# A fused attention and gated-MLP kernel: strided tile statistics, bias rows on another queue, operand sums in other places

## The chip, the cores and the metric

The kernel runs on one core of a Trainium2 chip. Its time is the device time of one launch in microseconds (us), taken as the median of several runs. A core has TensorE (PE, matrix products; PEld are its weight loads), VectorE (DVE), ScalarE (ACT), GpSimd (POOL) and SyncE (SP). Each has its own queue of instructions and takes them in order. ScalarE and SyncE also issue transfers (DMAs) from their queues: a transfer that must wait holds up whatever stands behind it on that engine. Engines wait for each other through semaphores.

## The reference

Two blocks with residuals, on x of 2048 tokens by 1024:

```python
h  = x + A(layernorm(x))          # 32 heads, 4 segments of 512 tokens, causal softmax in a segment,
                                  # plus a memory of the earlier segments, mixed by sigmoid(beta); then wo
h2 = h + B(layernorm(h))

def B(x):                         # F = 3584, Fh = 1792
    z  = gelu(x @ w_in)           # 2048 x 3584
    z1 = z[..., :Fh]
    z2 = layernorm(z[..., Fh:])   # over the 1792 features of a token
    g  = einsum('ts,sf->tf', w_sp, z2) + b_sp[:, None]     # w_sp is 2048 x 2048
    return (z1 * g) @ w_out       # 1792 x 1024
```

All inputs and the output are bf16. The change touches block B and nothing of A.

## The kernel before

**How it is built.** All operations go through a recorder (class _Recorder). It keeps the program's order on each engine and finds the waits itself: for each operand it looks up the cells of memory that it covers, 32 bytes of a partition each in SBUF (GRAN = 32), a whole bank of 2 KB in PSUM, and lets an instruction wait for the last writer or the readers of each cell. So two small tensors in one cell wait for each other though they share no byte, and a bank of PSUM is given back only when its reader has ended. There is no scheduler: the order of the Python calls is the order on each engine.

**Memory.** One arena holds everything at hand-chosen offsets. The first bytes hold constants of the attention (an identity at 0, an index table at 256, beta and gates from 768), dead after it; from there on small tensors of block B are laid out one after another (b3): ZST, ZMV, ZRS (statistics of z2, one entry for each tile of 128 tokens), SQ, SQZ, SQY (maxima or sums of squares for the f16 scales), TOT and TOP (scratch of a scale), SC and INV (a scale and its inverse), BSQ (squares of the bias rows).

**Stages of block B**, with their place in the profiled execution:

1. z2 (about 320 to 405 us). z2_group computes 128 tokens by 448 features of z; z2_gelu (ScalarE) writes it, z2_stats (VectorE) takes its statistics, and after the fourth part of a tile bn_aggr writes ZMV and GpSimd makes the inverse deviation ZRS by a power. The list todo gives the order of the groups; at(q, ...) hangs other work on the q-th group: sums of squares of w_sp (sp_norm), maxima of the weights of z1 (wz_norm), a scale (scale_of(1)), f16 copies of these weights (wz_half), and operand sums (hn_sum, sz_sum).
2. z1 (405 to 492 us). The product is done by Strassen's scheme in Winograd's form with two halves in each direction, 7 products for 8. Its operands are f16 and some are sums of blocks: hn_sum (VectorE, tensors HT, in the profile ht or z1x) of the activations, sz_sum (GpSimd, sz) of the weights. z1_step(g, k) is one product, g from 0 to 13 and k from 1 to 7; a list sorted by offs runs them in the order k = 6, 5, 1 of the next g, 7, 2, 3 of the last g, 4. on(g, k, ...) hangs other work on a step: z2_apply (normalises a tile of z2), scale_of(0) (the scale of w_sp), loads of w_sp (sp_load), f16 copies (sp_part), operand sums t1, t2, t3 (sp_sum).
3. First gating stage, gate(0), 492 to 577 us: the product of the first 1024 rows of w_sp with z2 by the same scheme, for g from 0 to 6 two columns of 128 features. p1 and p2 are the two products of one block of the result, the others accumulate in the banks bb and bc; stt (VectorE) reads a bank, scales, adds the bias, out multiplies by z1. s_sum makes operand sums of z2, copy1 (ScalarE) and two sums on GpSimd make the parts that several blocks share.
4. Output of the first 1024 tokens (577 to 633 us): 16 units of 128 tokens by 512 columns, 14 matmuls each. fin_load brings the residual into one of four buffers FIN; out_unit adds the product (fin on VectorE) and stores it. Both transfers are on ScalarE's queue, and the load for unit n + 2 waits for the store of unit n - 2 from the same buffer. Beside the units VectorE prepares w_sp for the second stage (sp_half, sp_sum), ScalarE squares w_out (wo_norm, in the profile t4h) and the bias rows (brow_sq, t4h too), and from the sums of squares come two scales: scale_y (YS, INVY) and scale_w (SCW, INVO). Each is a matmul of SQB with ones (total), a reduction on VectorE, a power on GpSimd and some operations of one column.
5. Second gating stage, gate(1), 633 to 719 us, as the first, for the other 1024 rows; each1(g, k) hangs the operands of the last stage on it: ScalarE's scaled copies of w_out (ob_scale) and VectorE's sums of them (ob_sum t1, t2, t3).
6. Output of the second 1024 tokens (719 to 767 us), again by the scheme: o_prod are the products, y_sum the operand sums sy of the gated values, o_adds GpSimd's sums of residual and shared part (ot), o_stt VectorE's reads of the banks. For g = 0 most of y_sum is done at the end of gate(1) for six of seven features; the last feature (lo = 6) follows when the last block is there.

**Lines that the steps touch:**

```python
        q.dma_start(FIN[k][:, 0:w], out2d[tc * 128:(tc + 1) * 128, lo:lo + w])     # fin_load
        if n == 9:
            brow_sq()
            scale_y()
            pool.tensor_copy(SQB[:, 0:8], SQY[:, 0:8])
        if n == 11:
            scale_w()
```

In this loop unit n's load, products, add and store are issued first, then wo_norm(n - 1) for n from 1 to 8, then the work of that n. In gate, each block g issues: products t2 and t1, stt of t2's bank, s_sum 4, 1 and 2, p1, each(g, 0), product t3, p2, each(g, 1), two stt, out, s_sum 3, stt and out of the next block's p1 and p2, product t4, each(g, 2), stt, out, product b22, stt, out, each(g, 3).

## Time and profile before

| | before |
|---|---|
| median of 13 runs | 768.63 us (761.83 to 770.74) |
| profiled execution: whole time | 768.99 us |
| profiled execution: span from first to last instruction | 767.3 us |
| mean granted TensorE clock | 0.996 |
| VectorE busy, 570 to 586 / 640 to 680 / 700 to 720 us | 9.01 of 16 / 36.46 of 40 / 18.86 of 20 |
| GpSimd busy, 390 to 420 us | 26.88 of 30 |

A time here is where something lies in the span. In rows of the timeline the number in brackets is the idle time of the engine just before the instruction, and behind the arrow what ended it. An instruction's duration as shown for TensorE includes about 0.16 us in which the next one already runs: products of 8 matmuls start every 1.73 us and are shown with 1.89. All operations bear the line of the recorder's helper (L210), so groups are told apart by tile names: zt are the sums of z1, tmp_u and tmp_s1b those of the gating stages, ss, sy, t1h to t4h, ht and sz operand sums, fin the output units.

### The profile page before, as it was taken

How to read it: one execution, taken by the hardware profiler on the slowest of the kernel's cores; microseconds unless marked ns; L12 is line 12 of the kernel's file. 1: busy time of each engine (PE TensorE's matmuls, PEld its weight loads, DVE VectorE, ACT ScalarE, POOL GpSimd, SP SyncE). 2: the span in 40 equal slices, each digit the busy share in tenths (PEclk: the TensorE clock that was granted, in tenths of full speed). 3: DMA queues.
4: the chain of work that ended last, by engine and by line, in shares of the span. 5: the costliest groups of instructions: out<-in, count | busy, mean ns of one | idle time of the engine just before them, and what ended most of it. 6: DMA issues, size and time to landing. Idle time of an engine off the chain costs nothing.

```text
span 767.3 us, 13442 instructions
## 1 busy us (share of the span) xinstructions
PE 748.0 (97%) x5401; PEld 358.2 (47%) x5470; DVE 576.5 (75%) x1016; ACT 422.9 (55%) x519; POOL 294.7 (38%) x447
## 2 busy tenths in 40 slices
PE   8999999999999999999999999999999979999898
PEld 4445555555454455455554444444444434444344
DVE  5586589768974675759866986998882755999986
ACT  6777877787777778146975789532230615300000
POOL 2574556555653333100079987412120001212242
PEclk9999999999999999999999999999999989999999
DMA  9654556353425231887620054500039830001111
GB/s 303 171 154 90 97 77 132 83 98 85 97 57 132 77 74 42 222 215 229 194 83 1 0 102 84 143 1 1 1 74 210 245 109 8 0 1 56 62 49 56
DMA packets 136784, 75.09 MB, mean 98 GB/s; under 512 B 98065, under 2 KB 126481, under 8 KB 136721
## 3 DMA queue, kind: packets, MB, share of 16 engines
q1 hardware_dynamic: 129472, 67.40, 36.2%
q10 hardware_dynamic: 7248, 6.82, 3.3%
q8 instruction: 43, 0.70, 0.4%
q14 instruction: 21, 0.16, 0.1%
HBM read 42.74 MB, written 8.39 MB: 67 GB/s over the span
## 4 chain that ended last, share of the span: by engine, by line
PE 75%; DVE 15%; issue 4%; POOL 3%; DMA 2%; ACT 1%; ACTq 0%; DVEq 0%; POOLq 0%
PE ps L210 75%; DVE tmp_u L210 2%; DVE z1x L210 2%; DVE ss L210 2%; DVE stats L210 1%; DVE zt L210 1%; POOL sz L210 1%; POOL zrs L210 1%; DMA out_dram<-fin 1%; DMA wv<-in_A_wv_dram 1%; DVE hch L210 1%; DVE sy L210 1%; DVE otok L210 0%; DVE fin L210 0%; DVE pqk L210 0%
## 5 line engine op out<-in xcount | busy, mean ns | idle before, releaser
L210 ACT ACTIVATE e<-ps 128x2048 bf16<-128x2048 f32 (+1 forms) x96 | 152.7, 1590 | 41.7 <-PE ps L210 41.5
L210 POOL TENSOR_SCALAR_AFFINE_SELECT e<-e 128x512 bf16<-128x512 bf16 x128 | 90.6, 720 | 131.9 <-ACT e L210 131.9
L210 PE MATMUL ps<-win,hnT 128*128 128x448 bf16 x512 | 98.4, 352 | 0.0
L210 POOL TENSOR_TENSOR tmp_s1b<-tmp_s,brow 128x512 f32<-128x512 f32 x28 | 33.9, 1212 | 133.8 <-DVE tmp_u L210 55.4
L210 PEld LDWEIGHTS ps<-win,hnT 128*128 128x128 bf16 x512 | 49.6, 98 | 46.3 <-issue 0.2
L210 PE MATMUL ps<-xnT,wk 128*128 128x512 bf16 x233 | 59.6, 380 | 1.2
L210 PE MATMUL ps<-wv,xnT 128*128 128x512 bf16 x255 | 59.4, 380 | 0.7 <-DMA wv<-in_A_wv_dram 0.4
L210 DVE TENSOR_TENSOR zt<-ps,zt 128x512 f32<-128x512 f32 x70 | 47.5, 687 | 15.3 <-PE ps L210 12.7
L210 PE MATMUL ps<-wo,oT 128*128 128x512 bf16 x254 | 57.7, 380 | 0.1
L210 PE MATMUL ps<-xnT,wq 128*128 128x512 bf16 x226 | 54.0, 379 | 1.6
L210 PE MATMUL ps<-w_out,z1T 128*128 128x512 bf16 x219 | 50.2, 390 | 0.3
L210 ACT ACTIVATE z<-ps 128x448 bf16<-128x448 f32 x60 | 30.8, 544 | 35.2 <-PE ps L210 35.2
L210 PEld LDWEIGHTS ps<-v,e 128*128 128x128 bf16 x1280 | 38.8, 96 | 14.0 <-issue 6.5
L210 DVE BATCH_NORM_STATS2 zst<-z 128x6 f32<-128x448 bf16 x64 | 37.8, 608 | 8.9 <-ACT z L210 8.8
L210 DVE RECIPROCAL rd<-ps 128x16 f32<-128x16 f32 x32 | 8.0, 250 | 47.1 <-PE ps L210 46.9
L210 PE MATMUL ps<-v,e 128*128 128x33 bf16 x1280 | 42.2, 178 | 0.0
L210 ACT ACTIVATE tmp_s<-ps,invy 128x512 f32<-128x512 f32 x7 | 4.8, 687 | 67.3 <-POOL tmp_s1b L210 36.9
L210 ACT ACTIVATE z1T<-zt,inv 128x512 bf16<-128x512 f32 x42 | 29.7, 719 | 16.2 <-DVE zt L210 16.1
L210 PEld LDWEIGHTS ps<-wo,oT 128*128 128x128 bf16 x256 | 24.1, 98 | 27.5
L210 PEld LDWEIGHTS ps<-xnT,wk 128*128 128x128 bf16 x256 | 22.6, 98 | 29.9 <-issue 5.0
L210 POOL TENSOR_TENSOR sz<-wzh 128x512 f16<-128x512 f16 x28 | 33.3, 1189 | 8.2 <-PE ps L210 8.2
L210 PEld LDWEIGHTS ps<-wv,xnT 128*128 128x128 bf16 x256 | 23.1, 98 | 27.5 <-DMA wv<-in_A_wv_dram 1.0
(206 smaller groups left out, 1484.2 us busy)
## 6 DMA issues: line engine op xcount, KB each, us to landing
sj<-in_B_w_sp_dram SPq DMA_DIRECT2D x16, 512.0 KB, 3.5
xch<-in_A_x_dram SPq DMA_DIRECT2D x16, 256.0 KB, 3.7
xr<-in_A_x_dram SPq DMA_DIRECT2D x16, 256.0 KB, 3.9
out_dram<-hch SPq DMA_DIRECT2D x16, 256.0 KB, 2.4
win<-in_B_w_in_dram SPq DMA_DIRECT2D x4, 896.0 KB, 5.4
wz<-in_B_w_in_dram SPq DMA_DIRECT2D x6, 512.0 KB, 7.5
wo<-in_A_wo_dram SPq DMA_DIRECT2D x1, 2048.0 KB, 8.6
fin<-out_dram ACTq DMA_DIRECT2D x16, 128.0 KB, 3.2
```

The costliest lines, as they stand in the source:

```text
L210: ins = getattr(e, op.name)(*op.args, **op.kw)
```

## The change

Six edits, all in block B:

- ZMV and ZRS have one entry in every 32 bytes, so each tile has cells of its own. ZRS, SQY and BSQ now lie over the dead constants.
- scale_of ends after the power; the three operations behind it become scale_end, called at group 25 for the weights of z1 as before, and for w_sp at step (2, 2), eight steps later than before.
- Operand sums on VectorE move: hn_sum t = 1 and 2 into the z2 stage, t = 3 and 4 to the steps k = 6 of g = 4 to 7; sp_sum t1 and t3 to other steps of g = 10 to 13.
- brow_load(1) is issued on ScalarE's queue ahead of the loads of the second half of w_out; before it stood on SyncE's behind 16 transposing loads of w_sp. brow_sq moves from unit 9 to 6, scale_y from 9 to 7, the copy to SQB from 9 to 10, scale_w from 11 to 12.
- In gate(1), p1(2) is issued inside block 0. The sums ob_sum, now with t4, all stand at each(g, 0), three in blocks 1 to 3 and 6, two in 4 and 5. Before, t1 to t3 stood two to a block at each(g, 0) and each(g, 3), and t4 in the last stage.
- The three small y_sum for the last feature run on GpSimd, ahead of o_adds(0). The first t1 product of the last stage is no longer split.

```diff
     ZST = b3("zst", [128, NTC, 4, 6], F32)
-    ZMV = b3("zmv", [128, NTC, 2], F32)
-    ZRS = b3("zrs", [128, NTC], F32)
+    ZMV = b3("zmv", [128, NTC, 8], F32)
+    ZRS = tens("zrs", [128, NTC * 8], F32, 256)
     ZNM = b3("znm", [128, 1], F32)
...
     TW, YS, INVY, SCW, INVO = [b3(k, [128, 1], F32) for k in ("tw", "ys", "invy", "scw", "invo")]
-    SQY = b3("sqy", [128, 28], F32)
-    BSQ = b3("bsq", [128, 2], F32)
+    SQY = tens("sqy", [128, 28], F32, 768)
+    BSQ = tens("bsq", [128, 2], F32, 896)
     TMP = {k: tens("tmp_" + k, [128, L], F32, (4 + 2 * i) * K)
...
         if k == 3:
-            dve.bn_aggr(ZMV[:, tc, :], ZST[:, tc, :, :])
-            pool.tensor_single_scalar(ZRS[:, tc:tc + 1], ZMV[:, tc, 1:2], float(LN_EPS), ALU.add)
-            pool.tensor_tensor(ZRS[:, tc:tc + 1], ZRS[:, tc:tc + 1], MHZ[:], ALU.pow)
+            dve.bn_aggr(ZMV[:, tc, 0:2], ZST[:, tc, :, :])
+            pool.tensor_single_scalar(ZRS[:, 8 * tc:8 * tc + 1], ZMV[:, tc, 1:2], float(LN_EPS), ALU.add)
+            pool.tensor_tensor(ZRS[:, 8 * tc:8 * tc + 1], ZRS[:, 8 * tc:8 * tc + 1], MHZ[:], ALU.pow)
             zq.append(tc)
...
         if on_act:
-            pool.tensor_scalar(ZNM[:], ZMV[:, tc, 0:1], ZRS[:, tc:tc + 1], -1.0, ALU.mult, ALU.mult)
-            act.activation(Z2H[:, tc, :], Z2[:, tc, :], ACTF.Identity, scale=ZRS[:, tc:tc + 1], bias=ZNM[:])
+            pool.tensor_scalar(ZNM[:], ZMV[:, tc, 0:1], ZRS[:, 8 * tc:8 * tc + 1], -1.0, ALU.mult, ALU.mult)
+            act.activation(Z2H[:, tc, :], Z2[:, tc, :], ACTF.Identity, scale=ZRS[:, 8 * tc:8 * tc + 1], bias=ZNM[:])
             return
-        dve.tensor_scalar(Z2H[:, tc, :], Z2[:, tc, :], ZMV[:, tc, 0:1], ZRS[:, tc:tc + 1], ALU.subtract, ALU.mult)
+        dve.tensor_scalar(Z2H[:, tc, :], Z2[:, tc, :], ZMV[:, tc, 0:1], ZRS[:, 8 * tc:8 * tc + 1], ALU.subtract, ALU.mult)
     LAST = NSEG * NQ - 1
...
             pool.tensor_tensor(TOP[:], TOT[:], MHZ[:], ALU.pow)
+
+    def scale_end(k):
         dve.tensor_single_scalar(TOP[:].bitcast(I32), TOP[:].bitcast(I32), 0x7F800000, ALU.bitwise_and)
...
     at(25, scale_of, 1, 14, None)
+    at(25, scale_end, 1)
     for k in range(8):
         at(26 + k, wz_half, k // 2, k % 2)
+    for k in range(4):
+        at(28 + 2 * k, hn_sum, 1, 1 + k // 2, k % 2)
     for k in (1, 2, 3, 4):
...
         p1(1)
-        p1(2)
+        if not pr:
+            p1(2)
         seam()
...
                 ss(2, g + 1)
-            if 1 <= g <= 3:
+            if 1 - pr <= g <= 3:
                 p1(g + 2)
...
         q.dma_start(out2d[tc * 128:(tc + 1) * 128, lo:lo + w], fin[:, 0:w])
-    def brow_load(pr):
+    def brow_load(pr, q=sp):
         for k in range(2):
             t = 1024 * pr + 512 * k
-            sp.dma_start(BROW[k][:], B_b_sp[t:t + 512].partition_broadcast(128))
+            q.dma_start(BROW[k][:], B_b_sp[t:t + 512].partition_broadcast(128))
     wout = B_w_out.rearrange("(c p) n -> p c n", p=128)
...
         on(g, 4, lambda: zq and z2_apply(True))
-    for k in range(8):
-        on((0, 1, 2, 3, 4, 4, 5, 5)[k], 3 if k < 5 else (7, 3, 7)[k - 5], hn_sum, 1, (1, 2, 3, 4)[k // 2], k % 2)
+    for k in range(4, 8):
+        on(*((4, 6), (5, 6), (6, 6), (7, 6))[k - 4], hn_sum, 1, (1, 2, 3, 4)[k // 2], k % 2)
     on(1, 7, scale_of, 0, 16, None)
+    on(2, 2, scale_end, 0)
     for k, g, r in (("b11", 6, 3), ("b12", 6, 3), ("b22", 8, 3), ("b21", 12, 3)):
...
     for r in range(4):
-        on(10 + r // 2, (3, 6, 3, 6)[r], sp_sum, "t1", r)
-        on(12 + r // 2, (3, 6, 3, 6)[r], sp_sum, "t3", r)
-        on(13, (5, 7, 2, 4)[r], sp_sum, "t2", r)
+        on(*((10, 6), (10, 5), (11, 6), (11, 5))[r], sp_sum, "t1", r)
+        on(*((12, 5), (12, 6), (13, 3), (13, 6))[r], sp_sum, "t3", r)
+        on(*((13, 5), (13, 7), (13, 2), (13, 4))[r], sp_sum, "t2", r)
     on(7, 3, brow_load, 0)
...
             sp_load(1, k, j)
-    brow_load(1)
+    brow_load(1, act)
     for i in range(2):
...
             wo_norm(n - 1)
+        if n == 6:
+            brow_sq()
+        if n == 7:
+            scale_y()
+        if n == 10:
+            pool.tensor_copy(SQB[:, 0:8], SQY[:, 0:8])
         if n == 1:
...
             sp_sum("t2")
-        if n == 9:
-            brow_sq()
-            scale_y()
-            pool.tensor_copy(SQB[:, 0:8], SQY[:, 0:8])
         if n == 10:
...
             sp_sum("t4")
-        if n == 11:
+        if n == 12:
             scale_w()
...
                     4: (y_blk(0, 1, g, lo, hi), y[:, 1, lo:hi, :], ALU.subtract)}[k]
-        if lo:
-            dve.scalar_tensor_tensor(o, a, 1.0, b, ALU.mult, op)
-        else:
-            dve.tensor_tensor(o, a, b, op)
+        (pool if lo else dve).tensor_tensor(o, a, b, op)
     def fin_in(g):
...
                 (1, 2): [(ob_scale, "b21", 0)], (1, 3): [(ob_scale, "b21", 1)], (6, 0): [(fin_in, 0), (fin_in, 1)]}
-        for n, (o, h) in enumerate([(o, h) for o in ("t1", "t2", "t3") for h in (0, 2, 4, 6)]):
-            jobs.setdefault((1 + n // 2, (0, 3)[n % 2]), []).append((ob_sum, o, h))
+        for n, (o, h) in enumerate([(o, h) for o in ("t1", "t2", "t3", "t4") for h in (0, 2, 4, 6)]):
+            jobs.setdefault(((1, 1, 1, 2, 2, 2, 3, 3, 3, 4, 4, 5, 5, 6, 6, 6)[n], 0), []).append((ob_sum, o, h))
         for f, *a in jobs.get((g, k), ()):
...
     o_p1(0)
-    o_adds(0)
     for x in range(1, 4):
         y_sum(x, 0, 6, 7)
+    o_adds(0)
     o_prod(3, o_s(2, 0), "t2", True, cs=range(6))
...
         f1, f12, f22, f21 = OT4[g % 2]
-        if g == 0:
-            o_prod(bc, o_s(1, g), "t1", True, cs=range(6))
-        cs = range(6, 7) if g == 0 else range(7)
-        o_prod(bb, o_s(2, g), "t2", True, cs=cs)
+        o_prod(bb, o_s(2, g), "t2", True, cs=range(7) if g else range(6, 7))
         for b, lo, hi in last:
-            o_prod(b, o_s(1, g), "t1", True, lo, hi, cs)
+            o_prod(b, o_s(1, g), "t1", True, lo, hi)
         o_stt(f12[:], bb, f12[:])
-        if g == 0:
-            ob_sum("t4", 0)
-            ob_sum("t4", 2)
-            ob_sum("t4", 4)
-            ob_sum("t4", 6)
         y_sum(4, g)
...
```

## The prediction

> **What bounds the kernel now.** I read the page's first part, then the table of waits for TensorE, then the chain of waits and the table by windows around the longest wait, and last the timeline of the places where VectorE is named. The page:
>
> ```profile
> PE 748.0 (97%) x5401; PEld 358.2 (47%) x5470; DVE 576.5 (75%) x1016; ACT 422.9 (55%) x519; POOL 294.7 (38%) x447
> ```
>
> TensorE is busy 748.0 of 767.3 us, and the change neither adds nor removes a large product (its matmuls are re-ordered, nothing more). So only TensorE's idle time, 19.3 us, can be won, plus time in which it runs at a lower clock. The waits of TensorE (us in total, times, longest):
>
> ```profile
> PE ps L210 <- POOL sqb L210: 5.4, 1, 5.4
> PE ps L210 <- DVE zt L210: 1.7, 3, 0.8
> ...
> PE ps L210 <- DVE tmp_u L210: 1.2, 3, 0.6
> PE ps L210 <- DVE sy L210: 1.0, 1, 1.0
> PE ps L210 <- DVE ot L210: 0.9, 1, 0.9
> ```
>
> One wait of 5.4 us, and four kinds of short ones. The rest of the 19.3 us lies at the start (2.4 before 20 us), in the first half, and behind the last matmul; the change touches none of that. The chain of waits, asked for 576 to 640 us, shows how the long one comes about:
>
> ```profile
> 607.62 0.69 DVE fin L210
> ...
> 608.34 6.46 DMA out_dram<-fin
> ...
> 615.74 0.07 ACT t4h L210
> ...
> 616.49 0.73 ACT t4h L210 x2
> ...
> 618.10 0.57 POOL top L210
> 618.67 0.16 POOL sqb L210
> ...
> 618.87 8.60 PE ps L210 x31
> ```
>
> Output unit 7 is stored at 608.34 and its store takes 6.46 us. ScalarE's next instruction is the load of unit 11 into the same fin buffer, so ScalarE stands until 614.8. Behind it in ScalarE's queue are the squares of the bias rows (t4h at 615.74 and 616.49), behind those GpSimd's power (618.10), and behind that, in GpSimd's queue, the copy to sqb (618.67), which the matmul of scale_w wants. By windows (us, then PE, PEld, DVE, ACT, POOL busy; clock; DMA):
>
> ```profile
> 613.00:614.00 1.00, 0.43 (x2) 0.00 (x0) 0.00 (x0) 0.00 (x0) 0.00 (x0) 1.00 1.08 381
> 616.00:617.00 1.00, 0.00 (x0) 0.00 (x0) 0.00 (x0) 0.97 (x3) 0.00 (x0) 0.51 0.73 236
> 621.00:622.00 1.00, 1.00 (x4) 0.44 (x3) 0.97 (x2) 0.00 (x0) 0.00 (x0) 0.50 0.58 163
> 622.00:623.00 1.00, 1.00 (x5) 0.32 (x4) 1.00 (x1) 0.00 (x0) 0.00 (x0) 0.58 0.10 33
> ```
>
> TensorE's work ends at 613.43; from 616.0 the granted clock is 0.5, and it comes back only near 622.6. The 3.7 us from 618.87 to 622.6 do 1.85 us of work. So the stall costs 5.4 + 1.85 = 7.3 us.
>
> The short waits, in the timeline:
>
> ```profile
> 484.79 1.48 DVE L210 TENSOR_TENSOR t1h<-b12h,b11h 128x1024 f16<-128x1024 f16 x1
> 487.52 1.04 PE L210 MATMUL ps<-ht,sz 128*128 128x512 f16 x4 [0.79 <-DVE zt L210]
> 690.48 1.90 PE L210 MATMUL ps<-t3h,ss 128*128 128x512 f16 x8 [0.42 <-DVE tmp_u L210]
> 723.56 1.24 DVE L210 SCALAR_TENSOR_TENSOR sy<-z1x 128x128 f16<-128x128 f16 x1
> 725.88 0.28 DVE L210 SCALAR_TENSOR_TENSOR sy<-z1x 128x128 f16<-128x128 f16 x1
> 727.40 2.21 DVE L210 TENSOR_TENSOR z2h<-w_out0h,z1x 128x1024 f16<-128x1024 f16 x4
> ```
>
> In each, a sum that is not urgent stands in VectorE's queue ahead of the read of a PSUM bank that TensorE wants back. The same sum is dearer while GpSimd works: 1.24 against 0.28 us.
>
> **What the Trainium skill says.** "TensorE: Matmul & The Clock Gate", section "What's actually happening": the clock is halved after an idle window of about 3.4 us and given back after a busy one; a note there adds that the window runs freely, so the point varies between runs. The trace agrees (0.5 from 2.6 us after the last matmul, full again 3.7 us after the restart), and one such stall more or less would explain why the 13 runs spread over 761.83 to 770.74. "GPSIMD Engine Reference", section "1. Specifications": GpSimd shares its SBUF interfaces with VectorE and contends with VectorE's instructions that have two SBUF inputs; the 1.24 against 0.28 us agrees. "DMA: Bandwidth & Descriptors", section "Queues, rings and completion order": ScalarE's and SyncE's transfers lie in a queue each, taken in order, and an engine takes packets of both in turn. The trace fits: the load of unit 2, issued on ScalarE behind the two w_out loads, reaches VectorE only at 594.94.
>
> **The change part by part.** Sums are made against the profiled execution, 768.99 us (span 767.3 and 1.7 around it), which is 0.36 above the median 768.63.
>
> *Second scale and bias rows.* The rows are loaded on ScalarE before w_out instead of on SyncE behind 16 transposes; the squares move from unit 9 to unit 6, scale_y to unit 7, the sqb copy to unit 10, scale_w from unit 11 to 12. ScalarE now squares the rows right after wo_norm of unit 6 (607.7), two times 0.75 us, to 609.2; from the last square to ys the old trace needs 1.85 us (617.2 to 619.05), so ys is there at about 611. Then come the two row copies (1.4), and wo_norm's last square (1.9) ends at about 614.5; GpSimd's copy needs 0.2. Unit 12 ends on TensorE at 613.43 + 3.07 = 616.5, so the matmul of scale_w doesn't wait: 7.3 us go. What is late next: VectorE now waits inside scale_y at unit 7, not in an idle stretch. From 611.2 it has the adds of units 8 to 14 (7 x 0.69), t2 2.29, b21 1.28, t4 2.29, three sums 2.07, the small operations of scale_w with GpSimd's power 1.9: 14.7 us, to 625.9. TensorE has finished unit 15 at 613.43 + 4 x 3.07 = 625.7 and needs bank 0, which unit 14's add frees: a wait of 0.2 at least. The rows put 256 KB ahead of w_out on ScalarE's queue (1 to 1.7 us at the 150 to 250 GB/s of that stretch), so everything that waited there until 594.9 comes 1 to 1.5 later, and the loads of units 9 and 10 fall into the transfer of 1.8 MB that starts at 607.4. I take 1.2, from 0.2 to 3. w_out's second half lands about 594.5 and is wanted at 596.8: hidden with 1 us left; uncovered it costs up to 1. SyncE's queue loses two issues of 0.5 us ahead of a load that waits for TensorE anyway: nothing. Net 6.1, from 4 to 7.
>
> *Statistics 32 bytes apart, scale_end, sums earlier.* VectorE's waits for GpSimd's zrs (0.9 + 3.2 us between 395 and 406) go, but TensorE is busy 10.00 of 10 us there: nothing by itself. scale_end puts the power's 1.13 us of waiting (before 417.41) behind other work, and four of eight sums ht move to 380 to 391, where they cost about 0.68 each and not up to 1.41; VectorE is 9.59 of 10 busy there, but has 4.2 us free from 390 to 400. This removes TensorE's idle time at 420.4 and 439.0: 0.29 + 0.45 + 0.34, some 1.1. Moving the t1 and t3 sums away from the last two blocks takes the 1.48 us at 484.79 out of the way of 487.52: 0.84. Sum 2.0, from 1 to 2.7.
>
> *Second gating stage.* p1(2) moves behind the first t1 product: VectorE then waits for the t3 product anyway (2.10 us idle before 645.21); nothing, plus or minus 0.3. The sums at the end of each block (just ahead of the read TensorE waits for: 0.42, 0.60 and 0.17 idle before t3) go to its start. But blocks 1 to 3 then carry three sums of 0.61 and no longer one or two. In block 1 VectorE was already 0.26 behind (657.47 against 657.21); with two more in that place the read ends at about 659.4 and the t4 product waits 0.6. Blocks 4 to 6 hold two, two and three. Followed instruction by instruction, VectorE needs 10.2 us and its sums per block, TensorE 12.1 in blocks 1 to 3 and 10.35 after: TensorE is about 0.2 us later than before at the end of block 6. A small loss, 1 either way.
>
> *End.* VectorE loses the three small sy sums (2.64 us with GpSimd beside them) and the four t4 sums (2.21). GpSimd now makes the small ones: its f16 sum of 128x512 takes 1.16, so a quarter of it and start-up give 0.35 to 0.5 each; the second is ready 0.9 us after VectorE's last z1x, about when TensorE asks for it. GpSimd's ot adds start 1.2 later than their inputs allow, and the first one (1.2) becomes the last to come before the t3 product: some 0.5. The t3 product, 727.53 before, comes at about 726.0 with the 0.2 taken in; t4 no longer waits for its operand either (0.3). Gain for stage and end together 1.9, from 0 to 3.
>
> Sum: 768.99 - 6.1 - 2.0 - 1.9 = 759.0.
>
> **Rivals.** (a) The stall goes, but half of its gain comes back at the seam: VectorE is 3 us or more behind when TensorE reaches p1(0), because the fin loads land late. For it: VectorE's 14.7 us of work in the 14.5 TensorE leaves. Against it: the store's 6.46 us no longer stand ahead of the squares. With a wait of 3 to 4 us and part of a half clock, 4.5 in all, and the short waits half as good: 768.99 - 2.8 - 2 = 764.2. (b) Only the long stall counts, the other parts come to nothing, since three sums in one block of a stage where VectorE is 97% busy make new waits: 768.99 - 6.1 - 0.5 = 762.4. (c) The seam uncovers nothing and the short waits vanish: 768.99 - 7.1 - 2.7 - 3 = 756.2. (d) Slower: ScalarE stands for a store between the squares and the row copies, VectorE stands in scale_y with all adds behind it, and TensorE stalls at p1(0) instead. One store of 6.46 held twice (12.9), less what is covered, and 3.3 of half clock: 768.99 - 7.3 + 16.2 - 3.9 = 774. It decides from a hold of about 12 us; at one store the sum is near 767.6. Against it: the loads ahead of unit 7's squares wait for stores issued at 603.6 and 604.5, which ended well before. (e) The new order doesn't move the copy to sqb ahead of scale_w: the order of instructions speaks against it; about 765.
>
> **How the numbers follow.** Forecast (757 to 761.5) 0.50; (b) 0.18; (a) 0.12; (c) 0.12; (e) and a one-store hold of (d), both no change, 0.05; (d) 0.03. Two runs of this kernel tell 0.5% (3.8 us) from no change, so faster means under 764.8. Forecast, (b), (c) and over half of (a) lie there, but the spread of the runs before may move the median: 0.83; within 0.14; slower 0.03. The range 755 to 764.5 takes in (c), (b) and most of (a).
>
> **What would show it.** Right: no wait for sqb above 0.5 us and clock 1.00 through 610 to 630; the squares about 8 us earlier; PE waits for zt under 0.7 in all; the t4 sums gone from the end. Wrong: a wait for fin at the first b11 product of the second stage above 2 us, or new waits for tmp_u at t4 products above 2 in sum.

## The result and the profile after

The changed kernel takes 758.68 us in the median of 11 runs (757.59 to 762.12). The kernel before, run again beside it and now with 48 runs, has a median of 766.43 us (761.83 to 774.16), so the ratio is 0.9901, with a 95% interval of 0.9875 to 0.9926: about 1% faster. The profiled execution took 759.11 us with a span of 757.4, against 768.99 and 767.3: 9.9 us less. The medians differ by 7.75 only, since the execution of before that was profiled is one of its longer ones. The experiments come back to this.

The page's first part and the waits of TensorE (us in total, times, longest) of the changed kernel:

```profile
PE 745.0 (98%) x5401; PEld 358.2 (47%) x5470; DVE 573.5 (76%) x1013; ACT 421.7 (56%) x519; POOL 294.1 (39%) x450
```

```profile
PE ps L210 <- DVE tmp_u L210: 1.5, 4, 0.6
PE ps L210 <- DVE etmp L210: 1.2, 1, 1.2
PE ps L210 <- DMA wv<-in_A_wv_dram: 1.2, 1, 1.2
PE ps L210 <- POOL sz L210: 1.0, 1, 1.0
PE ps L210 <- DVE ot L210: 0.4, 1, 0.4
```

The waits for sqb (5.4), zt (1.7) and sy (1.0) are gone. Those for tmp_u went from 1.2 to 1.5, and a wait for GpSimd's sz is new. The wait for wv lies at the start, before anything the change touches; two kernels below with the same start show 0.2 and 0.8 there, and the kernel before shows 0.4, so I take it as chance. The windows around the old stall (us, then PE, PEld, DVE, ACT, POOL busy; clock; DMA):

```profile
613.00:614.00 1.00, 1.00 (x6) 0.44 (x5) 0.00 (x0) 0.00 (x0) 0.00 (x0) 1.00 1.10 386
616.00:617.00 1.00, 1.00 (x6) 0.48 (x5) 0.97 (x2) 0.00 (x0) 0.00 (x0) 1.00 0.43 140
621.00:622.00 1.00, 1.00 (x6) 0.46 (x5) 0.72 (x5) 0.00 (x0) 0.14 (x1) 1.00 0.61 165
```

TensorE is busy throughout, at clock 1.00. The timeline of the same place shows the new order of the second scale (start, length, engine and operation, idle time before):

```profile
605.05 0.63 ACT L210 ACTIVATE t4h<-brow 128x512 f16<-128x512 bf16 x1
...
608.08 0.15 DVE L210 TENSOR_SCALAR top<-top 128x1 int32<-128x1 int32 x1 [2.15 <-POOL top L210]
...
612.28 0.19 POOL L210 CAST sqb<-sqy 128x8 bf16<-128x8 f32 x1 [4.24 <-ACT t4h L210]
...
614.84 0.69 DVE L210 TENSOR_TENSOR fin<-fin,ps 128x512 bf16<-128x512 bf16 x1 [2.81 <-DMA fin<-out_dram]
...
615.54 0.17 PE L210 MATMUL ps<-sqb,ones 128*128 128x8 bf16 x1
...
624.36 1.28 DVE L210 TENSOR_TENSOR fin<-fin,ps 128x512 bf16<-128x512 bf16 x2
```

The first square of the bias rows starts at 605.05 and no longer at 615.74 (9.9 us earlier when counted from the stage's first product, since the whole stage starts earlier too); sqb is ready 3.1 us before the product that reads it at 615.54. VectorE pays in two places, 2.15 us inside scale_y and 2.81 us for a late fin load, and neither reaches TensorE.

Stage lengths, read from TensorE's timeline as the distance between the first products of successive stages (the sums z1 with its operands, the first gating stage, the output units with the second scale, the second gating stage), and for the end to the span's end. In both of these profiles the record of the first product of z1 and of the output units is missing, and the next one, 0.2 us later, stands in its place; so up to z1 and the first gating stage are 0.2 too long in both columns, z1 and the output units 0.2 too short, and the differences stand:

| us | before | after | difference |
|---|---|---|---|
| up to z1 | 405.01 | 405.60 | +0.59 |
| z1 | 86.84 | 85.80 | -1.04 |
| first gating stage | 85.35 | 85.05 | -0.30 |
| output units | 55.72 | 48.18 | -7.54 |
| second gating stage | 86.31 | 87.00 | +0.69 |
| end | 48.07 | 45.77 | -2.30 |
| span | 767.3 | 757.4 | -9.9 |

In the tables below, where these two profiles stand beside others, the 0.2 is put right: z1 takes 87.05 before and 86.01 after, the output units 55.9 before and 48.4 after.

### The profile page after: what moved, and what is told of

Its sections match the earlier page's. It is cut to its first block, busy times and chain, and to the rows that moved or that the text cites. A ratio compares the mean times of both kernels' runs of the same rounds, so it can differ in the third digit from the quotient of the medians.

```text
span 757.4 us, 13417 instructions
## 1 busy us (share of the span) xinstructions
PE 745.0 (98%) x5401; PEld 358.2 (47%) x5470; DVE 573.5 (76%) x1013; ACT 421.7 (56%) x519; POOL 294.1 (39%) x450
## 4 chain that ended last, share of the span: by engine, by line
PE 73%; DVE 17%; DMA 3%; ACT 3%; POOL 2%; issue 2%; ACTq 0%; DVEq 0%; POOLq 0%
PE ps L210 73%; DVE z1x L210 3%; DVE tmp_u L210 3%; DVE ss L210 2%; ACT sj L210 2%; DMA sj<-in_B_w_sp_dram 2%; DVE stats L210 1%; POOL zrs L210 1%; DMA wv<-in_A_wv_dram 1%; POOL sz L210 1%; DVE zst L210 1%; DVE hch L210 1%; ACT z L210 1%; DVE tmp_s1b L210 1%; DVE wzh L210 1%
## 5 line engine op out<-in xcount | busy, mean ns | idle before, releaser
L210 PE MATMUL ps<-w_out,z1T 128*128 128x512 bf16 x219 | 48.1, 379 | 0.3
L210 DVE BATCH_NORM_STATS2 zst<-z 128x6 f32<-128x448 bf16 x64 | 38.0, 612 | 10.2 <-ACT z L210 10.2
```

What stands on the lines that cost most here:

```text
L210: ins = getattr(e, op.name)(*op.args, **op.kw)
```

## The experiments

All kernels below compute the whole output. Stage lengths are from their profiles, one execution each, in the manner of the table; a median stands with its number of runs. The kernels of one group ran on one chip with shared runs of the kernel before; the three groups ran on three chips, and medians are compared inside a group only. The indented texts are what was expected before the kernel ran. In them e1 is the kernel with the whole part, e8 the one with the old steps of ht, and f1 and f2 are the first and second of the last group's three new kernels.

### The order of the second scale against the queue of the bias rows

Four kernels, each the kernel before with a piece of one part of the change. The first has the whole part:

```diff
-    brow_load(1)
+    brow_load(1, act)
...
+        if n == 6:
+            brow_sq()
+        if n == 7:
+            scale_y()
+        if n == 10:
+            pool.tensor_copy(SQB[:, 0:8], SQY[:, 0:8])
...
-        if n == 9:
-            brow_sq()
-            scale_y()
-            pool.tensor_copy(SQB[:, 0:8], SQY[:, 0:8])
-        if n == 11:
+        if n == 12:
             scale_w()
```

> The kernel before with the bias-row edit alone (rows on ScalarE's queue, squares at unit 6, scale_y at 7, sqb at 10, scale_w at 12). Theory A (the squares stood behind a load that a store held, and the stall halved the clock): the output stage of the first half shrinks from 55.7 to 48.2 us, clock 1.00 from 610 to 630, time 7 under the profiled execution of before, about 761.5; ratio to before 0.990 to 0.995. Rival B (the profit is spread over all edits and the stage gives back part at the seam): 764 to 765.

The second has the order without the first two lines (the rows stay on SyncE's queue):

> The kernel before with the units of squares and scales moved as in the change, the rows left on SyncE's queue. Theory A (place in ScalarE's order decides): the rows landed about 604, the squares come at 605 to 608, so the long wait for sqb goes all the same: within 1 us of e1. Rival C (the rows come too late on SyncE, the queue decides): little or no gain, wait for sqb above 2 us stays.

The third has only the first two lines:

> The kernel before with the rows' loads on ScalarE's queue, all else as it was. Theory A: no gain, wait of TensorE for sqb as before (2 to 6 us), time within 1 us of before. Rival C: the gain of e1, wait under 0.5.

The fourth moves nothing but the squares, from behind the fin load issued in unit 9 to ahead of it:

```diff
     for n, u in enumerate(units):
+        if n == 9:
+            brow_sq()
         if n + 2 < 16:
...
         if n == 9:
-            brow_sq()
             scale_y()
```

> The kernel before with one call moved: at unit 9 the two squares are issued before the load of unit 11, not after it. Theory A: the squares start at 612.4 when wo_norm ends, ys and sqb are there 3.2 us later, near 615.7: TensorE waits 2.0 to 2.5 us instead of 5.4 and the clock stays at 1.00, so the stage takes 50.5 us and the time is 4 to 5 under the profiled execution of before. If the half clock doesn't hang on the length of the wait: 3 us less only.

| | output units, us | wait for sqb, us | median (runs) | range | ratio to before |
|---|---|---|---|---|---|
| whole part | 48.40 | none | 763.2 (20) | 761.19 to 764.97 | 0.9973 [0.9957, 0.9989] |
| order alone | 48.40 | none | 762.9 (20) | 761.25 to 765.15 | 0.9967 [0.9946, 0.9989] |
| queue alone | 49.45 | 0.9 | 765.39 (12) | 762.32 to 772.52 | 1.0027 [0.9995, 1.0059] |
| squares first | 50.55 | 2.0 | 764.96 (12) | 762.92 to 766.73 | 0.9997 [0.997, 1.0024] |
| before | 55.9 | 5.4 | 764.56 (55) | 761.43 to 772.32 | 1 |

(The row of before has its stage and wait from the one profile shown; its median and range are of the runs beside these four kernels.)

The order alone does all of it: 48.40 with and without the new queue. In the medians it gives less than the 0.990 to 0.995 expected, 0.9973 and 0.9967, for a reason that comes below. The new queue alone leaves the wait in place, though shorter in its profile. Two lines of ScalarE's timeline of that kernel say why it was shorter:

```profile
609.93 0.35 ACTq L210 DMA_DIRECT2D out_dram<-fin  x1
...
613.13 0.33 ACTq L210 DMA_DIRECT2D fin<-out_dram  x1
```

and the product that waits for sqb in TensorE's timeline:

```profile
617.34 0.18 PE L210 MATMUL ps<-sqb,ones 128*128 128x8 bf16 x1 [0.88 <-POOL sqb L210]
```

The load of unit 11 follows the store of unit 7 by 3.2 us here, and by 6.5 us (608.34 to 614.82) in the profile of before. The computing instructions stand in the same order as in before, so the length of the stall hangs on how long that store takes, and this differs between executions (whether the rows' new queue has a part in it, one execution can't say). The times of the runs fit: of the 55 runs of before 10 lie at 768.9 us or above, of the 12 with the queue alone three do (770.0, 771.3, 772.5), and of the 40 with the new order none is above 765.2. So do the clocks that the runs show: in 9 of these 55 and 3 of these 12 the mean clock is 0.996 or less, and they take 767.4 us or more; in all 40 with the new order it is 0.998 or 1.00. So the new order removes a long stall that only part of the runs have, and a shorter one otherwise. That explains why this part is worth 7.5 us in the profile shown, but 1.4 to 1.7 us between medians.

Squares first separates the wait from the clock. The product that reads sqb, and two windows (columns as above):

```profile
618.51 0.18 PE L210 MATMUL ps<-sqb,ones 128*128 128x8 bf16 x1 [1.98 <-POOL sqb L210]
```

```profile
617.00:618.00 1.00, 0.00 (x0) 0.00 (x0) 0.00 (x0) 0.00 (x0) 0.70 (x4) 1.00 1.08 383
...
619.00:620.00 1.00, 1.00 (x6) 0.47 (x5) 1.00 (x2) 1.00 (x2) 0.00 (x0) 1.00 0.35 116
```

ScalarE was held for the store as long as before (store issued at 611.13, load at 617.17: 6.0 us), but with the squares ahead of the load TensorE waits 2.0 us and not 5.4. The clock stays at 1.00 and the stage takes 50.55: 48.40 plus the wait of 1.98 and the overlap of 0.16 that it costs, and nothing more. Stage and wait came as expected (50.5; 2.0 to 2.5). The times did not: no gain between medians, and the profiled run, 766.73, is 2.3 us below that of before where 4 to 5 were expected, because z1 took 89.20 in it. So in this pair the longer wait brought the half clock and the shorter one didn't, and what stood behind the load, not the store itself, made the stall.

The length of one wait is not all that decides, though. In the profile of the queue alone the clock is 0.5 from 8.6 to 12.0 us, at the kernel's start, after a wait of only 1.36 us for wv with shorter gaps before it; the changed kernel waits 1.17 us in the same place, and its clock stays at 1.00.

### What the other parts are worth

Four kernels, each the changed kernel with one part taken back. The first has the operand sums of the second gating stage as before, two to a block at both ends of it, with t4 in the last stage:

```diff
-        for n, (o, h) in enumerate([(o, h) for o in ("t1", "t2", "t3", "t4") for h in (0, 2, 4, 6)]):
-            jobs.setdefault(((1, 1, 1, 2, 2, 2, 3, 3, 3, 4, 4, 5, 5, 6, 6, 6)[n], 0), []).append((ob_sum, o, h))
+        for n, (o, h) in enumerate([(o, h) for o in ("t1", "t2", "t3") for h in (0, 2, 4, 6)]):
+            jobs.setdefault((1 + n // 2, (0, 3)[n % 2]), []).append((ob_sum, o, h))
...
+        if g == 0:
+            for h in (0, 2, 4, 6):
+                ob_sum("t4", h)
```

> The changed kernel with the operand sums t1 to t3 of the last stage at both ends of the blocks as before and t4 in the last stage. Theory D (three sums in a block cost the second gating stage 0.7 us, t4's move pays 1 us at the end): second gating stage 86.3 us instead of 87.0, last stage 46.8 to 47.3 instead of 45.8, sum 0.3 to 0.8 worse. Rival E (the move only costs): last stage stays near 45.8, sum 0.7 better.

The second has the three small sums of the last feature on VectorE again, behind o_adds(0):

```diff
-        (pool if lo else dve).tensor_tensor(o, a, b, op)
+        if lo:
+            dve.scalar_tensor_tensor(o, a, 1.0, b, ALU.mult, op)
+        else:
+            dve.tensor_tensor(o, a, b, op)
...
+    o_adds(0)
     for x in range(1, 4):
         y_sum(x, 0, 6, 7)
-    o_adds(0)
```

> The changed kernel with the three small sy sums back on VectorE, behind GpSimd's ot adds as before. Theory D: VectorE needs 1.2 us for each of the first two beside GpSimd, a wait for sy of 0.8 to 1.5 us comes back, last stage 46.6 to 47.3 us. Rival E (only t4's move counts at the end): last stage within 0.3 of 45.8, since VectorE is free there now.

The third packs the statistics again (ZMV and ZRS with neighbouring tiles side by side; the indices that go with it are not shown):

```diff
-    ZMV = b3("zmv", [128, NTC, 8], F32)
-    ZRS = tens("zrs", [128, NTC * 8], F32, 256)
+    ZMV = b3("zmv", [128, NTC, 2], F32)
+    ZRS = tens("zrs", [128, NTC], F32, 256)
```

> The changed kernel with ZMV and ZRS packed as before (8 and 4 bytes a tile), so tiles share cells. Theory F (VectorE's waits for zrs lie beside full TensorE work): waits of VectorE for zrs of 2 to 5 us come back between 390 and 408, TensorE's waits in the z1 stage change by under 0.5, stage 85.5 to 86.5 us. Rival G (the separate cells are what saves z1): z1 stage above 87 us.

The fourth has the eight sums ht at their old steps:

```diff
-    for k in range(4):
-        at(28 + 2 * k, hn_sum, 1, 1 + k // 2, k % 2)
...
-    for k in range(4, 8):
-        on(*((4, 6), (5, 6), (6, 6), (7, 6))[k - 4], hn_sum, 1, (1, 2, 3, 4)[k // 2], k % 2)
+    for k in range(8):
+        on((0, 1, 2, 3, 4, 4, 5, 5)[k], 3 if k < 5 else (7, 3, 7)[k - 5], hn_sum, 1, (1, 2, 3, 4)[k // 2], k % 2)
```

> The changed kernel with all eight ht sums of the second half in the z1 stage at their old steps. Theory F (the four early sums delay bn_aggr, so GpSimd starts its powers later and the sz sum is late by 1.0): the wait for sz falls below 0.5, waits for zt of 0.3 to 0.8 come back, z1 stage 85.3 to 86.5 us, no clear change. Rival H (the early sums are where z1 gains): z1 stage above 87 us.

| us | z1 | second gating stage | end | span | median (runs) |
|---|---|---|---|---|---|
| changed kernel (its own runs, another chip) | 86.01 | 87.00 | 45.77 | 757.4 | 758.68 (11) |
| old operand sums | 86.01 | 86.31 | 48.11 | 758.7 | 759.69 (8) |
| small sums on VectorE | 86.01 | 86.98 | 47.15 | 757.5 | 760.12 (7) |
| packed statistics | 86.80 | 87.03 | 45.76 | 758.4 | 760.0 (10) |
| old steps of ht | 85.50 | 86.98 | 45.76 | 755.7 | 758.02 (4) |

*Old operand sums.* The end takes 2.34 us more and the second gating stage 0.69 less. The move of the sums is worth 1.65, and it costs something where they went. More was at stake than the 0.3 to 0.8 expected: the end was put at 46.8 to 47.3 and took 48.11, as long as in the kernel before (48.07).

*Small sums.* VectorE's timeline and the product that waits, in the kernel with the small sums on VectorE:

```profile
713.54 1.13 DVE L210 SCALAR_TENSOR_TENSOR sy<-z1x 128x128 f16<-128x128 f16 x1
714.70 1.12 DVE L210 SCALAR_TENSOR_TENSOR sy<-sy,z1x 128x128 f16<-128x128 f16 x1
...
715.88 1.90 PE L210 MATMUL ps<-z1x,sy 128*128 128x512 f16 x8 [1.05 <-DVE sy L210]
```

and in the changed kernel, where GpSimd makes them:

```profile
714.86 0.43 POOL L210 TENSOR_TENSOR sy<-z1x 128x128 f16<-128x128 f16 x1 [11.54 <-DVE z1x L210]
715.37 0.43 POOL L210 TENSOR_TENSOR sy<-sy,z1x 128x128 f16<-128x128 f16 x1
...
715.94 1.89 PE L210 MATMUL ps<-z1x,sy 128*128 128x512 f16 x8
...
718.20 1.68 PE L210 MATMUL ps<-z1x,sy 128*128 128x512 f16 x7 [0.37 <-DVE ot L210]
```

1.1 us each on VectorE beside GpSimd's adds, 0.43 on GpSimd; the product finds sy ready. This part is worth 1.38 us of the end. The second wait, 0.37 for ot, is the price that stays: the ot adds start behind the small sums. The two parts together would make 3.7 us of an end that is 2.30 shorter in all, so they don't add: with the old operand sums the end is as long as before though GpSimd makes the small sums, which pay only where the operand sums have moved.

*Packed statistics.* VectorE's timeline there, and TensorE's, have waits that the changed kernel doesn't:

```profile
401.38 0.26 DVE L210 BATCH_NORM_AGGREGATE zmv<-zst 128x2 f32<-128x24 f32 x1 [2.51 <-POOL zrs L210]
...
403.34 0.26 DVE L210 BATCH_NORM_AGGREGATE zmv<-zst 128x2 f32<-128x24 f32 x1 [1.21 <-POOL zrs L210]
```

```profile
410.26 1.04 PE L210 MATMUL ps<-z1x,sz 128*128 128x512 f16 x4 [1.06 <-DVE zt L210]
```

The statistics of one tile wait for GpSimd to have read those of its neighbour, and the read of a bank behind them comes late. The stage takes 86.80, against 85.16 to 86.01 in the six profiles with separate cells and ht sums in the z2 stage (this table and the next, median 86.0). So the cells are worth about 0.8 us here. Neither theory had this: the stage lies between F's 86.5 and G's 87, and TensorE has a new wait of 1.06 where F wanted changes under 0.5.

The same wait stands in two of the five kernels with the old z2 and z1 stages, 0.50 at 409.07 (the whole part of the second scale) and 0.94 at 410.32 (squares first), and in none of the other three. What sets the two groups apart is how early the statistics are. The seventh bn_aggr comes 9.5, 9.0 and here 9.2 us before the first product of z1 where TensorE waits, and 11.4, 11.4 (before, order alone) and 10.5 us (queue alone) where it doesn't. So packed cells cost nothing in an execution with room ahead of z1, as that of before, and 0.5 to 1.1 us where the statistics are late; the ht sums in the z2 stage are one thing that makes them late, as the next kernel shows.

*Old steps of ht.* The wait for sz is gone, one of 0.3 for zt is back (0.32 at 437.76), and the stage is 85.50, inside the 85.16 to 86.01 of the six: the early sums bring nothing that these profiles can tell. The theory of the text above holds here. The seventh bn_aggr comes 10.4 us before the first product of z1, in the changed kernel 8.8, and GpSimd's first sum sz, which stands behind that tile's power, 9.2 against 7.6. The new wait in the changed kernel is

```profile
412.70 1.90 PE L210 MATMUL ps<-z1x,sz 128*128 128x512 f16 x8 [1.01 <-POOL sz L210]
```

Early ht sums are not the only way to it: with old ht steps and packed cells it is 0.55, 0.20 and 0.55 in the whole part of the second scale, the queue alone and squares first.

### A better version, and why sz is late

Four kernels on one chip: the changed kernel again, as the measure for three with more changes.

> The changed kernel itself, on the chip of the three that follow: 758 to 759.5, stages z1 85.5 to 86.2, second gating stage 87.0, last stage 45.8.

The first of the three moves operand sums into block 0 of the second gating stage, where VectorE had room:

```diff
-        jobs = {(0, 0): [(ob_scale, "b11", 0)], (0, 1): [(ob_scale, "b11", 1)], (0, 2): [(ob_scale, "b12", 0)],
-                (0, 3): [(ob_scale, "b12", 1)], (1, 0): [(ob_scale, "b22", 0)], (1, 1): [(ob_scale, "b22", 1)],
-                (1, 2): [(ob_scale, "b21", 0)], (1, 3): [(ob_scale, "b21", 1)], (6, 0): [(fin_in, 0), (fin_in, 1)]}
+        jobs = {(0, 0): [(ob_scale, "b11", 0), (ob_scale, "b12", 0)], (0, 1): [(ob_scale, "b11", 1), (ob_scale, "b12", 1)],
+                (0, 2): [(ob_scale, "b22", 0)], (1, 0): [(ob_scale, "b22", 1)], (1, 1): [(ob_scale, "b21", 0)],
+                (1, 2): [(ob_scale, "b21", 1)], (6, 0): [(fin_in, 0), (fin_in, 1)]}
...
-            jobs.setdefault(((1, 1, 1, 2, 2, 2, 3, 3, 3, 4, 4, 5, 5, 6, 6, 6)[n], 0), []).append((ob_sum, o, h))
+            at_g = (0, 0, 0, 0, 1, 2, 2, 2, 3, 3, 3, 4, 5, 5, 6, 6)[n]
+            jobs.setdefault((at_g, 0 if at_g else 1), []).append((ob_sum, o, h))
```

> The changed kernel with the scaled copies and the four t1 sums of the last stage moved into block 0 of the second gating stage, where VectorE stands idle 3.8 us before its t3 read, and the rest thinned (1, 3, 3, 1, 2, 2 sums in blocks 1 to 6). Theory D (the waits of the stage come from more sums than a block holds): the wait of 0.49 at block 1's t4 product goes and the later ones shrink, second gating stage 84.9 to 86.0 us instead of 87.0. Rival I (VectorE's own 10.2 us per block set the pace from block 4 on): 86.3 to 87.

The second adds to this an ot add ahead of the third small sum, and four ht sums eight groups later:

```diff
-        at(28 + 2 * k, hn_sum, 1, 1 + k // 2, k % 2)
+        at(36 + 2 * k, hn_sum, 1, 1 + k // 2, k % 2)
...
-    for x in range(1, 4):
-        y_sum(x, 0, 6, 7)
-    o_adds(0)
+    y_sum(1, 0, 6, 7)
+    y_sum(2, 0, 6, 7)
+    o_adds(0, (1,))
+    y_sum(3, 0, 6, 7)
+    o_adds(0, (2, 3))
```

> As f1, with the four early ht sums eight groups later in the z2 stage, and GpSimd's ot add for f12 ahead of the third small sy sum. Theory F: ht sums no longer delay the first powers, wait for sz under 0.5, z1 stage 85.0 to 85.5 us. Last stage 45.2 to 45.5 us, since the wait of 0.4 for ot goes. Sum 2 to 3 us under the changed kernel.

The third is the second with the ht sums at their old steps:

> As f2, but with all ht sums at their old steps in the z1 stage. Theory F: z1 stage 85.5 us as in e8, so within 0.4 us of f2. Rival H: z1 stage 0.5 or more above f2.

| us | z1 | second gating stage | end | span | median of 6 runs | ratio to before |
|---|---|---|---|---|---|---|
| changed kernel again | 85.71 | 87.35 | 45.76 | 757.2 | 758.82 | 0.9903 [0.9872, 0.9934] |
| sums into block 0 | 85.16 | 86.08 | 45.74 | 754.7 | 756.63 | 0.9878 [0.9844, 0.9911] |
| and ot add first, ht later | 86.00 | 85.45 | 45.30 | 754.2 | 756.68 | 0.9881 [0.985, 0.9913] |
| and ht at old steps | 85.51 | 86.06 | 45.27 | 754.8 | 756.17 | 0.9874 [0.9843, 0.9905] |

*Sums into block 0.* The second gating stage loses 1.3 us against the kernel on the same chip. That is 0.1 above the expected range and just below the rival's 86.3. All but one of its waits for tmp_u go (0.17 stays, at 695.09). A wait of 0.46 for ScalarE's tmp_s near the start of the stage stands beside it; it is 0.19 in the changed kernel on this chip, none in the second of the three, and 0.44 us before 627.53 in the last kernel:

```profile
627.53 1.90 PE L210 MATMUL ps<-b21h,z2h 128*128 128x512 f16 x8 [0.44 <-ACT tmp_s L210]
```

*The ot add first* takes 0.44 off the end (45.74 to 45.30). *The ht sums later* were to bring bn_aggr forward on VectorE, and with it sz on GpSimd, so that the wait for sz is under 0.5 and z1 takes 85.0 to 85.5. Both were missed: the wait is still 1.0, the stage 86.00. The first half of the reason holds all the same. Four figures in six profiles, the first two in us before the first product of z1:

| | seventh bn_aggr | GpSimd's first sz sum | from it to the fifth | wait for sz |
|---|---|---|---|---|
| changed kernel | 8.8 | 7.6 | 12.4 | 1.0 |
| changed kernel again | 9.1 | 7.8 | 12.4 | 0.7 |
| sums into block 0 | 9.4 | 8.2 | 12.2 | 0.2 |
| and ot add first, ht later | 10.3 | 8.8 | 13.7 | 1.0 |
| and ht at old steps | 10.4 | 9.2 | 12.2 | none |
| changed kernel, old steps of ht | 10.4 | 9.2 | 12.2 | none |

In the three with the early sums as changed, bn_aggr and GpSimd's chain behind it are late by 1.0 to 1.6 us, and the wait follows that lateness. With the sums eight groups later bn_aggr is back, but GpSimd itself takes longer. Its timeline there:

```profile
394.28 0.53 POOL L210 TENSOR_SCALAR zrs<-zmv 128x1 f32<-128x1 f32 x1 [0.58 <-DVE zmv L210]
...
396.84 1.06 POOL L210 TENSOR_TENSOR zrs<-zrs,mhz 128x1 f32<-128x1 f32 x1
...
399.13 0.65 POOL L210 TENSOR_SCALAR zrs<-zmv 128x1 f32<-128x1 f32 x1
...
401.52 0.66 POOL L210 TENSOR_SCALAR zrs<-zmv 128x1 f32<-128x1 f32 x1
...
409.08 1.15 POOL L210 TENSOR_TENSOR sz<-wzh 128x512 f16<-128x512 f16 x1
```

VectorE's ht sums in the same stretch:

```profile
396.86 0.63 DVE L210 TENSOR_TENSOR ht<-hnT,hnT 128x1024 f16<-128x1024 bf16 x1
...
399.02 0.69 DVE L210 TENSOR_TENSOR ht<-hnT,ht 128x1024 f16<-128x1024 bf16 x1
...
401.29 0.81 DVE L210 TENSOR_TENSOR ht<-hnT,ht 128x1024 f16<-128x1024 bf16 x1
```

and GpSimd in the changed kernel with the old steps of ht:

```profile
396.42 0.56 POOL L210 TENSOR_TENSOR zrs<-zrs,mhz 128x1 f32<-128x1 f32 x1
398.21 0.22 POOL L210 TENSOR_SCALAR zrs<-zmv 128x1 f32<-128x1 f32 x1
...
407.17 1.42 POOL L210 TENSOR_TENSOR sz<-wzh 128x512 f16<-128x512 f16 x1
```

The same one-column operations take 1.06 against 0.56 and 0.53 to 0.66 against 0.22 us where an ht sum lies beside them (the first of four such sums starts at 394.11), and the sum sz that begins at 407.17 in the one begins at 409.08 in the other (the next sum of the pair is what TensorE waits for). The four shown are 1.7 us longer, of the 1.9 that sz is late, and GpSimd works almost without a pause from 395 to 412. So this fits; but no run takes the lengthening alone away, and it stays a likely cause and not a shown one.

The best version, the last one, takes 756.17 us (755.76 to 757.56), 2.65 us or 0.35% less than the changed kernel's 758.82 on the same chip. It is within the 0.4 expected of the second (756.68), as theory F had it. Between it and "sums into block 0" the medians differ by less than their ranges, so the changes after the first are not shown to pay in the whole time.

## Why the prediction was right

The forecast was 759.0 us, and 758.68 came. The sum holds by its signs and its largest term, the stall. Its other terms were off by 0.3 to 1.4 us either way and partly cancel, so that the time came within 0.3 us is in part luck.

- **The stall of the second scale.** As predicted: no wait for sqb, clock 1.00, the squares 10.7 us earlier, 9.9 counted from the stage's start (about 8 were foretold). The 7.3 us of stall and half clock went; the stage is 7.54 us shorter. By finer windows the half clock lasts from 616.0 to 622.8, and with the overlap of 0.16 the stall costs 7.6 us, which is the same. Rival (e) is out. One reading was wrong without harm: ScalarE doesn't stand from the store at 608.34 to 614.8. Two squares of w_out, a load and a store come between, and it stands idle only from 612.35 to 614.82; the load of unit 11 still holds the squares of the rows until then. Of the prediction's two reasons to move things, only the order counted; the stage is as long with the rows' old queue. The sum rests on the one profiled execution; 7.3 is the price of its long stall, and a typical run of before pays less, as the runs of the order alone show. Hence a gain of 10.0 us was foretold from that execution, and between the medians it is 7.75 (6.6 on the chip of the last group). The forecast of the time after does not suffer from this, because that time has no stall.
- **The seam: a mis-sized term.** The prediction gave back 1.2 us there, because p1(0) was thought to need bank 0 from unit 14's add. VectorE's work was sized well: it ends at 625.64, foretold 625.9. But TensorE starts the stage at 624.63, while that add is still running:

```profile
624.63 3.62 PE L210 MATMUL ps<-b11h,z2h 128*128 128x512 f16 x16
```

Counted over in the order in which banks are handed out, unit 14's bank is not the one that p1(0) takes. p1(0)'s bank last held unit 9, p1(1)'s unit 10, and those were added long before. So the seam costs nothing, and rivals (a) and (d), which needed VectorE's lateness there, had no ground. The late fin load that (a) built on is there (2.81 us at 614.84), and VectorE absorbs it.

- **z2 and z1.** Foretold 2.0, from 1 to 2.7. The two profiles differ by 1.04, but this stage spreads: 87.03 to 89.20 in the five profiles with its old form (median 87.7), 85.16 to 86.01 in the six with the new one (median 86.0), so 1.7 is the better figure. In the pair, what was to go went: the named waits at 420.4, 439.0 and 487.52 were 0.64, 0.28 and 0.79 us, which with 0.16 of overlap each makes 2.2. Against it stands the new wait for sz, 1.01 and 0.16, which nobody foretold; 1.0 is left. Where each gain comes from is shown in part. The wait at 439.0 comes back with the old ht steps (0.32), so it belongs to these sums. Those at 420.4 and 487.52 stand in all five profiles with the old form and in none of the nine with the new one, also not with packed cells or old ht steps; that leaves scale_end and the moves of t1 and t3, as the prediction had it, but neither was taken back by itself. The step that was wrong in part is "nothing by itself" for the separate cells: it fits the execution of before, where the statistics are early, but VectorE's delay reaches TensorE where they are late, and then it costs 0.5 to 1.1.
- **The first gating stage** was put at nothing and is 0.3 shorter. In before one of TensorE's t3 products, at 514.58, starts 2.01 us after the one ahead of it and not 1.73, just when VectorE's read of its bank (513.76, 0.75 long) has ended; in the changed kernel that read ends at 513.71 and the product, at 513.84, isn't held. VectorE enters the stage 0.6 us earlier there, with fewer sums ahead. All five kernels with the old z1 stage have 85.1 in this stage, all nine with the new one 84.8, whatever the cells and the ht sums; so it comes with the t1 and t3 moves or scale_end.
- **The second gating stage.** Foretold 0.2 later, 1 either way; it is 0.69. The mechanism was right in its first place: three sums in block 1 ahead of the read that frees t4's bank, with a wait of 0.49 (0.6 foretold). VectorE's and TensorE's lines there, and the later waits:

```profile
648.58 1.89 DVE L210 TENSOR_TENSOR z1x<-z1x,w_out0h 128x1024 f16<-128x1024 f16 x3
650.38 0.75 DVE L210 SCALAR_TENSOR_TENSOR tmp_u<-ps,invy,tmp_s1b 128x512 f32<-128x512 f32 x1
```

```profile
651.18 1.90 PE L210 MATMUL ps<-t4h,z2h 128*128 128x512 f16 x8 [0.49 <-DVE tmp_u L210]
682.63 1.90 PE L210 MATMUL ps<-t3h,ss 128*128 128x512 f16 x8 [0.19 <-DVE tmp_u L210]
686.42 1.90 PE L210 MATMUL ps<-t4h,z2h 128*128 128x512 f16 x8 [0.17 <-DVE tmp_u L210]
694.15 1.90 PE L210 MATMUL ps<-t3h,ss 128*128 128x512 f16 x8 [0.65 <-DVE tmp_u L210]
```

The last three, 1.0 us in sum, were not foretold. The prediction took the waits of before ahead of t3 (0.42, 0.60 and 0.17) as gone; waits of the same size came in blocks 4 and 5. There the prediction's own figures say so: VectorE needs 10.2 us and two sums of 0.61, which is more than TensorE's 10.35. VectorE works there without a pause, 11.52 us for the block from 681.82 to 693.34, and TensorE's t3 products at 682.63 and 694.15 are 11.52 apart. The t4 products wait 0.66 in sum, well below the 2 that would have refuted the step. Rival (b) expected this stage to eat the small gains; it ate 0.7 of the 4.0 that z1 (1.7) and the end (2.3) brought.
- **The end.** Foretold for this stage and the end together 1.9, measured 2.30 less 0.69, that is 1.6. The small sums take 0.43 (0.35 to 0.5 foretold). The t3 product comes 6.57 us after the last stage's start (718.20 less 711.63); foretold were 726.0 with a start 0.2 after 719.23, also 6.6. t4 doesn't wait.
- **What cancelled.** By the pair of profiles, 9.99 us were foretold and 9.88 came: the output units with the seam 1.4 better (7.54 for 6.1), z1 1.0 worse (1.04 for 2.0), the second gating stage with the end 0.3 worse, 0.6 lost at the start by chance, and 0.3 gained in the first gating stage.

## What to carry to other kernels

In this kernel a DMA issue that waited for an earlier store held everything behind it in ScalarE's queue. The remedy was to move the short computation that others need ahead of it in program order; moving its input to another queue left the wait. Before charging a seam for a busy engine, count which buffer the next stage really takes, and when that one was last used. A sum off the critical path was cheapest here where its engine had a gap inside the block, and not on average over it. Small operations on one engine took longer beside two-input sums on another, so price them from rows with the same neighbour. And when a wait is to be removed by an earlier place for some work, follow the chain that this work then delays: here it was the statistics and, behind them, sz.

## What the runs showed of the hardware

- 5.4 us of idle TensorE brought the clock to 0.5 for 6.8 us (616.0 to 622.8, from 2.6 us after the last matmul); a wait of 2.0 us in the same place left 1.00. In another kernel a wait of 1.36 us, with shorter gaps before it, brought 0.5 for 3.4 us (8.6 to 12.0). The Trainium skill, "TensorE: Matmul & The Clock Gate", "What's actually happening", has a window of about 3.4 us that runs freely. The lengths of the half clock, one and two such windows, agree with it; that a whole window must be idle first does not agree with 2.6 and 1.36 us.
- From the issue of unit 7's store to the load that waits for it took 3.2, 6.0 and 6.5 us in three executions with the same store. With the mean clocks of the runs, this fits much of the spread of the kernel before; how the stall is spread over its runs was not traced.
- The sharing of SBUF interfaces in "GPSIMD Engine Reference", "1. Specifications", agrees with what VectorE shows: its small sum takes 1.1 us beside GpSimd's adds (0.28 without, in the profile of before). GpSimd showed the like: its one-column operations took two to three times as long, 0.65 for 0.22 and 1.06 for 0.56 us, beside VectorE's f16 sums.
